# A written-out order for chunks 1 to 7 of a sort-attention and gated-MLP kernel, with seven units' scores and two value groups on 64 rows of TensorE

## Chip, cores, metric

One Trainium2 chip, one of its cores. The metric is the device time of one execution in microseconds (us), as the median of the runs shown. All matmul operands are bfloat16, all products are collected in float32 in PSUM, and the result is float32.

## What is computed

Attention over blocks that a Sinkhorn-normalized matrix has mixed, followed by a two-layer MLP with a gate. Cut to what matters:

```python
# q, k, v: (4, 8, 768, 64) = batch, heads, rows, width; sort_net: (4, 8, 8, 8)
P = sort_net
for _ in range(5):
    P = exp(P - P.max(-1)); P = P / (P.sum(-1) + 1e-9); P = P / (P.sum(-2) + 1e-9)
k_sorted = einsum('bhij,bhjcd->bhicd', P, k_blocks)     # 8 blocks of 96 rows
v_sorted = einsum('bhij,bhjcd->bhicd', P, v_blocks)
scores = (q_block @ k_sorted_block.T) / sqrt(64)        # 96 x 96 in each block and head
attn = softmax(scores)
x = attn @ v_sorted                                     # -> 3072 tokens x 512
h = x @ w_in                                            # 512 -> 2048
out = (h * cos(h)) @ w_out                              # 2048 -> 512
```

## The kernel before

**Chunks.** The 3072 tokens are worked off in 8 chunks of 384 (`TC`); chunk n is half of batch n // 2. A chunk has 4 units u of 96 tokens (one block of all 8 heads). Chunks 0 to 3 use the sorted keys and values of the first two batches (`kT`, `vS[0]`), chunks 4 to 7 those of the last two (`kT2`, `vS[1]`, which lies in the tile `pair`). While the MLP of chunk n runs, the attention of chunk n + 1 is put between its products. The sorted keys and values of the later batches are made in pieces between those products as well.

**The steps of one unit.** The scores are 8 matmuls (`scores`, L403, shown as L405), one for each head: the stationary operand is 128 columns of the transposed queries, the streamed one 96 columns of keys. Two heads share the 128 rows of a tile. `q_turned` holds each head's 64 rows with zeros in the other 64, so every matmul uses all 128 rows. VectorE (DVE) takes the maximum (L447) and subtracts it (L449; chunk 1 uses L698 and L702). ScalarE (ACT) takes the exponential into one of three buffers `p_bufs` (`expo`, L462, shown as L467). The result is transposed, on TensorE in chunks 0 and 1 and for one unit of chunk 2, else by a DMA that SyncE's queue (SP) issues (L480), into `pT`. Then come 8 value products (`av_products`, L502, shown as L514), the division by the row sums on DVE (`av_norm`, L525 and L527), and a second transposition into `xT`, on TensorE (L545) or by SP's DMA (L533). A half-score (`qk_half`) is the same for one head of each pair, 4 matmuls.

**The MLP of one chunk.** `up` (L551) makes 2 of 16 row groups of h with 8 matmuls of 384 columns (L558); ACT computes cos (L562), DVE multiplies (L566). 8 such steps are one chunk. `down` (L578) then makes the 128-token output tiles ts = 0, 1, 2 with 16 matmuls of 512 columns each (L583); a half is 8 of them, and some work is put behind the fourth one of a half (`mid`).

**Sorting.** `k_sort_g` (L378) makes 4 column groups of the late keys with 4 matmuls (L375) and one copy. `v_sort_b` (L411) makes 8 columns of the values of batch 1 (L415); `v_sort_g` (L422) makes 4 or 8 columns of the last two batches' values (L425: 128 rows, 128 streamed columns each), and a copy puts them into `vS[1]`. `k_swap` (L387) moves half of the keys to the other 64 rows by two DMAs of SP's queue; the scores of chunk 2 need those of the first swap, and the scores of chunk 4 need those of the second.

**What sets the order.** The pools run under `tc.manual_schedule()`: each engine does its instructions in the order in which the program emits them, and each waits by semaphores for what it reads and for the buffer that it writes. PSUM has three buffers of two banks (pool `big`: up, full scores, value products, most transposes) and two of one bank (pool `acc`: output tiles, half-scores, most sorting). A new tile needs a buffer whose last reader is done. In the code from L782 the calls of chunk 0 and of the attention of chunk 1 stand one by one; from L981 on, helpers with slots (`moe_up`, `moe_down`, `ahead`) emit a step of the MLP and then what is listed for its slot. In these helpers the parts of a step are bound together: `qk` emits scores, maximum and subtraction in one go, `up` its products, cosine and gate, `av` the products and the division.

GpSimd (POOL) issues the loads, permutes the value columns (`v_permute`, L169) and has three "holds" (L484, L393): one-element copies that make the loads behind them wait for an earlier reader.

Of the kernel before, what the change touches and what calls it, by code (L numbers as in the profile page):

```python
# [14 lines left out]
AX = mybir.AxisListType  # L15


@with_exitstack
def kernel(
# [15 lines left out]
    nc = tc.nc  # L35
# [336 lines left out]
    MH = H2 * IC  # L372

    def k_products(ps, t, c, rows, rhs, keys=kbuf):
        nc.tensor.matmul(  # L375
            ps[:, t], keys[rows, c * 2 * D:(c + 1) * 2 * D], rhs, start=True, stop=True)

    def k_sort_g(t0, eng, pool, tag):  # L378
        ps = pool.tile([128, 4, 4 * NB], FP32, name="ks", tag=tag)
        for t in range(4):  # L380
            k_products(ps, t, t0 + t, slice(0, 128), bds[1].rearrange("p x i -> p (x i)"),
                       pair)
        copy_on(
            eng, kT2[:, ::2, :, :, t0:t0 + 4].rearrange("p e b m t -> p b e m t"),
            ps.rearrange("p t (b e m) -> p b e m t", b=2, e=2))

    def k_swap(keys):  # L387
        nc.sync.dma_start(out=keys[:64, 1], in_=keys[64:, 0])
        nc.sync.dma_start(out=keys[64:, 1], in_=keys[:64, 2])

    def hold_keys():

        nc.gpsimd.tensor_copy(held[:], kT[1][:, 1, 0, :1])  # L393
# [14 lines left out]
    def v_cols(d, permuted):  # L408
        return vperm[:, d * blk:d * blk + 128] if permuted else vv[:, d]

    def v_sort_b(b, d0, nd, eng, pool, tag):  # L411
        ps = pool.tile([128, nd, 2 * NB], FP32, name="vs", tag=tag)
        rows, xs = slice(0, 64 + b * 64), slice(b * H, (b + 1) * H)
        for t in range(nd):
            nc.tensor.matmul(  # L415
                ps[:, t], v_cols(d0 + t, b == 1 or d0 + t >= D // 2)[rows],
                bdv[rows, xs].rearrange("p x i -> p (x i)"), start=True, stop=True)
        copy_on(
            eng, vS[0][:, b * 2 * NB:(b + 1) * 2 * NB, d0:d0 + nd],
            ps[:blk].rearrange("p t n -> p n t"))  # L420

    def v_sort_g(d0, nd, eng, pool, tag):  # L422
        ps = pool.tile([128, nd, 4 * NB], FP32, name="vs", tag=tag)
        for t in range(nd):
            nc.tensor.matmul(  # L425
                ps[:, t], v_cols(d0 + t, True), bds[1].rearrange("p x i -> p (x i)"),
                start=True, stop=True)
        copy_on(eng, vS[1][:, :, d0:d0 + nd], ps[:blk].rearrange("p t n -> p n t"))

    def v_at(g, b2, hp, h2, i):  # L430
        return (b2 * 2 + hp) * NB + h2 * nb + i


    LATE = 5
    s_t, pb, pT, xn_t = {}, {}, {}, {}
    xT = {}
    cnt = [0]

    def qk_part(n, u, part, pool, tag):
        w = len(part)  # L440
        sc = pool.tile([128, w, 512], FP32, name="sc", tag=tag)
        for h2 in range(H2):
            for e, hp in enumerate(part):
                scores(sc[:, e, h2 * 128:h2 * 128 + blk], n, u, h2, hp)
        scv = sc[:blk].rearrange("p e (h c) -> p (e h) c", c=128)[:, :, :blk]
        mx = small.tile([blk, w * H2], FP32, name="mx", tag="mx")
        nc.vector.reduce_max(mx[:], scv, axis=AX.X)  # L447
        s = s_t[n, u][:, part[0]:part[0] + w].rearrange("p e h c -> p (e h) c")
        nc.vector.tensor_tensor(s, scv, mx.to_broadcast(list(s.shape)), op=ALU.subtract)  # L449

    def qk(n, u):

        s_t[n, u] = sp.tile([blk, 2, H2, blk], FP32, name="s", tag="s")
        qk_part(n, u, [0, 1], big, "big")

    def qk_half(n, u, hp, pool=None, tag="acc"):

        if hp == 0:
            s_t[n, u] = sp.tile([blk, 2, H2, blk], FP32, name="s", tag="s")
        qk_part(n, u, [hp], pool or acc, tag)  # L460

    def expo(n, u, on_pe=False):  # L462
        p = p_bufs[cnt[0] % NP]
        cnt[0] += 1


        nc.scalar.activation(  # L467
            p[:, :, :blk], s_t.pop((n, u)).rearrange("p e h c -> p (e h) c"), AF.Exp,
            scale=scale)
        if n < LATE:  # L470
            t = ptp.tile([128, 2 * H2, blk], BF16, name="pT", tag="pT")
        else:

            z, w = (n * IC + u) % 8, 2 * H2 * blk
            t = vperm[:, z * w:(z + 1) * w].rearrange("p (a c) -> p a c", c=blk)
        pT[n, u] = t
        if on_pe:
            pb[n, u] = p
        else:
            nc.sync.dma_start_transpose(out=t[:], in_=p.rearrange("p a c -> p (a c)"))  # L480

    def hold(t):

        nc.gpsimd.tensor_copy(held[:blk], t[:blk, 0, :1])  # L484

    def p_hold(n, u):
        hold(pT[n, u])

    def p_transpose(n, u, eng, pool, tag):
        p = pb.pop((n, u))  # L490
        ps = pool.tile([128, 2 * H2, 128], BF16, name="pps", tag=tag)
        for a in range(2 * H2):
            nc.tensor.transpose(ps[:blk, a, :blk], p[:, a, :blk], ident[:blk, :blk])
        copy_on(eng, pT[n, u][:blk], ps[:blk, :, :blk])

    av_ps = {}

    def av(n, u, on_pe=False):
        av_products(n, u)
        av_norm(n, u, on_pe)  # L500

    def av_products(n, u):  # L502
        g, b2, ih = where(n)
        if n not in xT:
            xT[n] = xtp.tile([128, KC, TC], BF16, name="xT", tag="xT")
        a = big.tile([128, 2, 512], FP32, name="av", tag="big")
# [12 lines left out]
        av_ps[n, u] = a  # L519

    def av_norm(n, u, on_pe=False):
        avv = av_ps.pop((n, u))[:blk, :, :H2 * (D + 1)].rearrange(
# [3 lines left out]
        xn = small.tile([blk, H2, 2, D], BF16, name="xn", tag="xn")  # L526
# [3 lines left out]
        if on_pe:  # L530
            xn_t[n, u] = xn
        else:
            nc.sync.dma_start_transpose(  # L533
                out=xT[n][:, :, u * blk:(u + 1) * blk],
                in_=xn.rearrange("p h e d -> p (h e d)"))

    def x_transpose(n, u, eng, pool, tag, to=None):
        us = range(u, (u if to is None else to) + 1)
        ps = pool.tile([128, KC, len(us), blk], BF16, name="xps", tag=tag)

        turn = order[:] if n < NQ else ident[:blk, :blk]
        for i, z in enumerate(us):
            xn = xn_t.pop((n, z))
            for h2 in range(H2):
                nc.tensor.transpose(  # L545
                    ps[:, h2, i], xn[:, h2].rearrange("p e d -> p (e d)"), turn)
        copy_on(eng, xT[n][:, :, u * blk:us.stop * blk], ps.rearrange("p k i c -> p k (i c)"))

    gt = {}

    def up(n, fp):  # L551
        w = TC

        h = big.tile([128, 2, 512], FP32, name="h", tag="big")
        for f2 in range(2):
            f = fp * 2 + f2
            for kk in range(KC):
                nc.tensor.matmul(  # L558
                    h[:, f2, :w], w_in_t[:, kk, f * 128:(f + 1) * 128], xT[n][:, kk],
                    start=(kk == 0), stop=(kk == KC - 1))  # L560
        c = cosp.tile([128, 2, TC], FP32, name="c", tag="c")
        nc.scalar.activation(c[:], h[:, :, :w], AF.Sin, bias=half_pi[:, 0:1])  # L562
        if fp % 2 == 0:
# [576 lines left out]
```

## Time and profile before

| | |
|---|---|
| median of 3 runs | 238.28 us (238.25, 238.28, 240.16) |
| span of the profiled execution, first to last instruction | 236.9 us |
| median less span | 1.4 us |
| TensorE (PE) busy | 228.3 us, 96% of the span |
| VectorE busy | 171.1 us, 72% |
| ScalarE busy | 154.0 us, 65% |
| GpSimd busy | 93.4 us, 39% |
| matmuls | 2230 |
| read from and written to HBM | 27.27 MB, 6.29 MB |
| granted TensorE clock, mean of the span | 0.998 |

The profiled execution has no time of its own beside its span; what lies around the span is 1.4 us if it ran as the median did. In the profile, a matmul's row shows when it started and when its last result is taken to be written, so matmuls in a row overlap in time. What one costs in a row of them is the distance between starts. "Idle" of PE is therefore less than what is lost: a pause shorter than a matmul's tail is not seen as idle. The chain of waits cuts the overlap out and is the better place to read the cost of a group of matmuls.

### The profile page before, as it was taken

The page shows a single profiled execution, that of the slowest core. Times are in us where ns is not written, and L with a number is a line of the kernel's source. Part 1 is how long each engine was busy: PE and PEld are TensorE (multiplying, and loading weights), DVE is VectorE, ACT ScalarE, POOL GpSimd, SP SyncE. Part 2 cuts the span into 40 slices and gives each one's busy share as a digit, 9 for nine tenths or more (in the row PEclk, how much of TensorE's full clock was granted, in tenths as well). Part 3 has the DMA queues.
Part 4 walks back from the last instruction along what each step waited for, and adds up shares of the span by engine and source line. Part 5 has one row for each costly group of instructions (what it writes and reads, how often), then busy time and mean ns, then how long its engine had stood idle before and what let it go on. Part 6 is the DMA issues. An engine that isn't in the chain of part 4 may idle for free.

```text
span 236.9 us, 5429 instructions
## 1 busy us (share of the span) xinstructions
PE 228.3 (96%) x2230; PEld 144.0 (61%) x2230; DVE 171.1 (72%) x284; ACT 154.0 (65%) x205; POOL 93.4 (39%) x117
## 2 busy tenths in 40 slices
PE   8699999999999999999999999999999999999994
PEld 2368799567665656655666556655564565555553
DVE  5658976887789666893689976998698769535700
ACT  3356975588889747795688747673767376646611
POOL 7699994894970098940808000800000000000000
PEclk9999999999999999999999999999999999999999
DMA  7999999995899989869899938944972460341012
GB/s 97 203 199 205 203 224 211 148 201 167 102 117 183 146 155 136 160 150 184 95 104 101 116 64 150 209 68 91 119 216 46 80 192 3 55 133 47 0 44 89
DMA packets 66423, 30.89 MB, mean 130 GB/s; under 512 B 55136, under 2 KB 61920, under 8 KB 66144
## 3 DMA queue, kind: packets, MB, share of 16 engines
q0 software_dynamic: 24048, 13.64, 42.1%
q1 hardware_dynamic: 42064, 16.73, 33.4%
q8 instruction: 17, 0.28, 0.5%
q10 hardware_dynamic: 288, 0.20, 0.3%
q14 instruction: 6, 0.05, 0.1%
HBM read 27.27 MB, written 6.29 MB: 142 GB/s over the span
## 4 chain that ended last, share of the span: by engine, by line
PE 81%; DMA 6%; ACT 4%; DVE 4%; issue 3%; POOL 1%; SPq 0%; ACTq 0%; POOLq 0%
PE h L558 31%; PE o L583 21%; DMA pT<-p_buf 5%; PE h L735 5%; PE o L756 4%; PE sc L405 3%; PE av L514 3%; PE ks L375 2%; PE vs L662 2%; ACT p_buf L467 2%; PE o L1104 1%; PE vs L425 1%; PE pps L713 1%; DMA xT<-xn 1%; PE vs L238 1%
## 5 line engine op out<-in xcount | busy, mean ns | idle before, releaser
L558 PE MATMUL h<-xT,w_in_t 128*128 128x384 bf16 x448 | 78.4, 326 | 0.2 <-DMA xT<-xn 0.2
L583 PE MATMUL o<-w_out_t,gg 128*128 128x512 bf16 x320 | 76.5, 379 | 0.0
L566 DVE TENSOR_TENSOR gg<-c,h 128x768 bf16<-128x768 f32 x56 | 52.6, 949 | 18.8 <-ACT c L562 18.8
L562 ACT ACTIVATE c<-h,half_pi 128x768 f32<-128x768 f32 x56 | 50.4, 900 | 22.5 <-PE h L558 21.6
L558 PEld LDWEIGHTS <-w_in_t 128*128 128x128 bf16 x448 | 42.2, 98 | 26.5 <-issue 0.6
L583 PEld LDWEIGHTS <-gg 128*128 128x128 bf16 x320 | 29.1, 98 | 27.6
L467 ACT ACTIVATE p_buf<-s 96x768 bf16<-96x768 f32 x32 | 26.0, 840 | 4.4 <-DVE s L702 2.4
L179 POOL COPY vperm<-kv 64x1536 bf16<-64x1536 bf16 (+1 forms) x10 | 28.0, 2831 | 0.6 <-DMA kv<-in_v_dram 0.6
L449 DVE TENSOR_TENSOR s<-sc,mx 96x384 f32<-96x384 f32 (+1 forms) x33 | 24.3, 735 | 1.8
L447 DVE TENSOR_REDUCE mx<-sc 96x4 f32<-96x384 f32 (+1 forms) x33 | 24.0, 729 | 0.7 <-PE sc L405 0.7
L527 DVE TENSOR_TENSOR xn<-av,r 96x512 bf16<-96x512 f32 x32 | 22.0, 687 | 1.1
L525 DVE RECIPROCAL r<-av 96x8 f32<-96x8 f32 x32 | 6.4, 199 | 14.6 <-PE av L514 14.4
L129 POOL DMA_DIRECT2D kv<-in_q_dram x24 | 15.9, 674 | 0.7 <-issue 0.5
L405 PE MATMUL sc<-kTs,q_turned 128*128 128x96 bf16 x224 | 15.3, 206 | 0.1
L249 ACT COPY kv<-o 128x512 f32<-128x512 f32 (+2 forms) x10 | 5.3, 530 | 14.9 <-PE o L583 12.4
L405 PEld LDWEIGHTS <-q_turned 128*128 128x128 bf16 x224 | 12.6, 98 | 4.0 <-DVE s L449 0.4
L249 ACT CAST kTs<-ks 128x512 bf16<-128x512 f32 (+1 forms) x18 | 11.0, 632 | 5.7 <-PE ks L375 5.7
L756 PE MATMUL o<-w_out_t,gg 128*128 128x512 bf16 x48 | 11.4, 379 | 0.0
L251 DVE COPY kv<-o 128x512 f32<-128x512 f32 (+1 forms) x5 | 3.0, 602 | 11.4 <-PE o L1104 8.5
L129 POOL DMA_DIRECT2D q_mem<-in_q_dram x16 | 10.7, 684 | 1.2 <-DMA kv<-in_v_dram 1.0
L238 PE MATMUL idle<-warm 128*128 128x512 bf16 x29 | 8.5, 436 | 2.8 <-ACT q_turned L321 1.8
L735 PE MATMUL h<-xT,w_in_t 128*128 128x192 bf16 x128 | 11.1, 246 | 0.0
(119 smaller groups left out, 285.0 us busy)
## 6 DMA issues: line engine op xcount, KB each, us to landing
out_dram<-kv SPq DMA_DIRECT2D x12, 256.0 KB, 2.5
out_dram<-o_s SPq DMA_DIRECT2D x10, 256.0 KB, 2.7
w_in_t<-in_moe_w_in_dram POOLq DMA_DIRECT2D x4, 512.0 KB, 11.8
w_out_t<-in_moe_w_out_dram POOLq DMA_DIRECT2D x4, 512.0 KB, 12.6
kv<-in_k_dram POOLq DMA_DIRECT2D x2, 768.0 KB, 10.3
kv<-in_v_dram POOLq DMA_DIRECT2D x2, 768.0 KB, 13.1
pair<-in_k_dram POOLq DMA_DIRECT2D x2, 768.0 KB, 11.0
kv<-in_v_dram POOLq DMA_DIRECT2D x6, 256.0 KB, 5.4
```

The lines of the kernel that those rows point to most:

```text
L129: nc.gpsimd.dma_start(out=q_heads[:, i, :, e], in_=src[:, ih * IC + i, :, e])
L179: nc.gpsimd.tensor_copy(dst, src)
L405: nc.tensor.matmul(out, q_of(n, hp)[:, x:x + 128], keys_of(n, u, h2, hp), start=True, stop=True)
L447: nc.vector.reduce_max(mx[:], scv, axis=AX.X)
L449: nc.vector.tensor_tensor(s, scv, mx.to_broadcast(list(s.shape)), op=ALU.subtract)
L467: nc.scalar.activation(p[:, :, :blk], s_t.pop((n, u)).rearrange("p e h c -> p (e h) c"), AF.Exp, scale=scale)
L527: nc.vector.tensor_tensor(xn.rearrange("p h e d -> p e h d"), avv[:, :, :, :D], r.to_broadcast([blk, 2, H2, D]), op=ALU.mult)
L558: nc.tensor.matmul(h[:, f2, :w], w_in_t[:, kk, f * 128:(f + 1) * 128], xT[n][:, kk], start=(kk == 0), stop=(kk == KC - 1))
L562: nc.scalar.activation(c[:], h[:, :, :w], AF.Sin, bias=half_pi[:, 0:1])
L566: nc.vector.tensor_tensor(gt[n, fp // 2][:, f:f + 2], c[:], h[:, :, :w], op=ALU.mult)
L583: nc.tensor.matmul(o[:], gt[n, f // 4][:, f % 4, ts * 128:(ts + 1) * 128], w_out_t[:, f, :], start=(f == 0), stop=(f == FC - 1))
L735: nc.tensor.matmul(o[:, part, f2 * w:(f2 + 1) * w], w_in_t[:, kk, f * 128:(f + 1) * 128], xT[0][:, kk, h * w:(h + 1) * w], start=(kk == 0) ...
```

## The change

Chunk 0 and all that is emitted before its output products stays. What follows is no longer emitted by helpers with slots, but by a list, `PLAN`, of one word for each piece of work: S scores, M maximum, X subtraction, E exponential (with the number of its buffer), TD transposition by DMA, TP and TE by TensorE and its copy, AV and N value products and division, XD, XP and XE the second transposition, U, C, G an up step's products, cosine and gate, D a quarter (4 matmuls) of an output tile, O its copy out of PSUM, W its store, kg/kge, vb/vbe, vg/vge the sorting products and their copies, kswap and QD the swaps and query transposes on SP's queue, Lq, Lpv and hp/hq the loads and holds on POOL. "B" and "c" name the pools `big` and `acc`, "A" and "V" the engine of a copy; "nop" does nothing. The pieces of one step can so be set apart, and pieces of other steps between them.

- The order of the DMAs on SP's queue and of everything on POOL is the old one, word for word. The set of pieces is the old one but for the points below. The order on PE, VectorE and ScalarE is changed in many places from the output products of chunk 0 on; the first are chunk 1's maxima and sums, the last is up step 6 and 7 of chunk 7.
- `T` takes the place of `S` for the scores of seven units: (3,3), (4,3), (5,0), (6,0), (6,1), (7,2), (7,1). Each head's matmul uses its own 64 rows alone, and the two heads of a pair alternate. (4,3) and (5,0), (6,0) and (6,1), (7,2) and (7,1) stand next to each other on PE.
- `vgT` takes the place of `vg` for the value groups 0 and 2 (8 columns each): 16 matmuls of 64 rows and 64 streamed columns in place of 8 of 128 and 128. They stand ahead of and behind unit (3,3), so that there are four places with 64-row products.
- Five copies change engine or pool: the copy of key group 0 (`kse 0`) and of value group 0 (`vge 0`) go from ScalarE to VectorE, `XE 3 1` and the output copy `O 5 2` change engine (VectorE to ScalarE), and `XP 3 2` goes from `big` to `acc`.

```diff
+    def T(n, u, pool, tag):
+        o = kept_tile(("s", n, u, None), pool, tag, [128, 2, 512], FP32, "sc")
+        for h2 in range(H2):
+            for hp in range(2):
+                rows, x = slice(hp * D, (hp + 1) * D), (u * H2 + h2) * blk
+                nc.tensor.matmul(
+                    o[:, hp, h2 * 128:h2 * 128 + blk], q_of(n, hp)[rows, x:x + 128],
+                    keys_of(n, u, h2, hp)[rows], start=True, stop=True)
...
+    def vgT(z, nd, pool, tag):
+        o = kept_tile(("vg", z), pool, tag, [128, 2, nd, 2 * NB], FP32, "vs")
+        for t in range(nd):
+            for b in range(2):
+                rows = slice(b * 64, (b + 1) * 64)
+                nc.tensor.matmul(
+                    o[:, b, t], v_cols(z * 4 + t, True)[rows],
+                    bds[1][rows, b * H:(b + 1) * H].rearrange("p x i -> p (x i)"),
+                    start=True, stop=True)
```

The orders on PE at the places of which the prediction speaks (the first: on the engine of the copy), before and after, in the words of the list; a word without a sign stands in both:

```diff
 kse 5 V                                  (key copies ahead of the first swap)
-kse 0 A
+kse 0 V
 kswap 0
...
 D 1 0 2                                  (output products of chunk 1)
-kg 0 c / D 1 0 3 / S 2 3 B / kg 1 B / D 1 1 0 / D 1 1 1 / kg 2 B / AV 2 0 / kg 4 B / D 1 1 2 / D 1 1 3
-kg 3 B / AV 2 1 / TP 2 3 c / D 1 2 0 / D 1 2 1 / AV 2 2 / XP 2 1 B / AV 2 3 / XP 2 0 c / D 1 2 2
+S 2 3 B / kg 0 c / D 1 0 3 / kg 1 B / D 1 1 0 / D 1 1 1 / kg 4 B / D 1 1 2 / AV 2 0 / kg 2 B / D 1 1 3
+kg 3 B / AV 2 1 / TP 2 3 c / AV 2 2 / D 1 2 0 / XP 2 1 B / D 1 2 1 / AV 2 3 / XP 2 0 c / D 1 2 2
 kg 5 B / XP 2 2 B / XP 2 3 B / D 1 2 3
...
 D 2 0 3                                  (output products of chunk 2)
-S 3 3 B / vg 0 8 B / D 2 1 0 / D 2 1 1 / vg 2 8 B / D 2 1 2 / D 2 1 3 / AV 3 0 / AV 3 1 / vg 4 8 B
-D 2 2 0 / D 2 2 1 / AV 3 2 / AV 3 3 / vg 6 8 B / D 2 2 2 / XP 3 1 B / XP 3 2 B / XP 3 3 B / D 2 2 3
-U 3 0 / vg 8 4 c / S 4 0 c 0 / U 3 1
+vgT 0 8 B / T 3 3 B / vgT 2 8 B / D 2 1 0 / D 2 1 1 / D 2 1 2 / D 2 1 3 / AV 3 0 / AV 3 1
+D 2 2 0 / AV 3 2 / D 2 2 1 / AV 3 3 / vg 6 8 B / D 2 2 2 / XP 3 1 B / XP 3 2 c / XP 3 3 B / D 2 2 3
+U 3 0 / vg 8 4 c / vg 4 8 B / U 3 1 / S 4 0 c 0
...
 S 4 2 B / D 3 0 0 / D 3 0 1              (output products of chunk 3)
-S 4 3 B / D 3 0 2 / D 3 0 3 / vg 15 4 B / S 5 0 B / D 3 1 0
+T 4 3 B / T 5 0 B / D 3 0 2 / D 3 1 0 / vg 15 4 B / D 3 0 3
 D 3 1 1 / AV 4 0 / D 3 1 2 / D 3 1 3 / AV 4 1 / AV 4 2 / D 3 2 0 / D 3 2 1 / XP 4 1 B 2 / AV 4 3
...
 D 4 0 0 / D 4 0 1                        (output products of chunk 4)
-S 6 0 B / D 4 0 2 / D 4 0 3 / AV 5 0 / D 4 1 0 / D 4 1 1 / S 6 1 B / D 4 1 2 / AV 5 1 / D 4 1 3 / AV 5 2
-D 4 2 0 / D 4 2 1 / AV 5 3 / S 6 2 B / D 4 2 2 / XP 5 3 B / D 4 2 3
+D 4 0 2 / T 6 0 B / T 6 1 B / D 4 0 3 / AV 5 0 / D 4 1 0 / D 4 1 1 / D 4 1 2 / AV 5 1 / AV 5 2 / D 4 1 3
+D 4 2 0 / AV 5 3 / D 4 2 1 / D 4 2 2 / XP 5 3 B / D 4 2 3 / S 6 2 B
 U 5 0
...
 D 5 1 0 / D 5 1 1 / AV 6 2               (output products of chunk 5)
-S 7 1 B / D 5 1 2 / D 5 1 3 / AV 6 3 / D 5 2 0 / D 5 2 1 / S 7 2 B / D 5 2 2 / XP 6 3 B / D 5 2 3
+T 7 2 B / T 7 1 B / D 5 1 2 / AV 6 3 / D 5 1 3 / D 5 2 0 / D 5 2 1 / XP 6 3 B / D 5 2 2 / D 5 2 3
```

On VectorE in chunk 4's output products the subtraction `X 6 1` moves behind the divisions `N 5 1` and `N 5 2`, and with it the exponential `E 6 1` on ScalarE. The loop at the end of the kernel (the last output tile of chunk 7) is unchanged.

1651 lines of the change are left out of this document (1083 added, 568 removed).

## The prediction, made before the change was run

> **What bounds the kernel now.** I read the page first (busy times, groups), then PE's own rows for pauses, then the chain of waits and SP's rows around each pause.
>
> ```profile
> span 236.9 us, 5429 instructions
> ...
> PE 228.3 (96%) x2230; PEld 144.0 (61%) x2230; DVE 171.1 (72%) x284; ACT 154.0 (65%) x205; POOL 93.4 (39%) x117
> ...
> L558 PE MATMUL h<-xT,w_in_t 128*128 128x384 bf16 x448 | 78.4, 326 | 0.2 <-DMA xT<-xn 0.2
> ```
>
> PE is the bound: 96% busy, and its largest group, the up products at 78.4 / 448 = 175 ns each, is neither shortened nor made smaller. So the change can win only pauses of PE and the few matmuls that it halves. A pause is the distance between two starts less the work between them (columns: start, length with its tail, instruction, count):
>
> ```profile
> 62.68 0.40 PE L415 MATMUL vs<-bdv,vperm 128*128 128x64 bf16 x8
> 63.18 0.33 PE L405 MATMUL sc<-kTs,q_turned 128*128 128x96 bf16 x4
> ...
> 74.89 1.03 PE L583 MATMUL o<-w_out_t,gg 128*128 128x512 bf16 x4
> 75.94 0.33 PE L375 MATMUL ks<-bd,pair 128*128 128x128 bf16 x3
> ...
> 86.27 0.34 PE L545 MATMUL xps<-order,xn 96*128 96x96 bf16 x4
> 86.87 0.34 PE L545 MATMUL xps<-order,xn 96*128 96x96 bf16 x4 [0.27 <-DVE xn L527]
> ...
> 91.13 1.46 PE L558 MATMUL h<-xT,w_in_t 128*128 128x384 bf16 x8
> 92.53 0.38 PE L375 MATMUL ks<-bd,pair 128*128 128x128 bf16 x4
> ...
> 108.91 0.68 PE L514 MATMUL av<-vS,pT 96*128 96x65 bf16 x16
> 109.94 0.61 PE L425 MATMUL vs<-bd,vperm 128*128 128x128 bf16 x8 [0.34 <-ACT pair L249]
> ...
> 113.93 0.91 PE L545 MATMUL xps<-ident,xn 96*128 96x96 bf16 x12
> 114.68 1.03 PE L583 MATMUL o<-w_out_t,gg 128*128 128x512 bf16 x4
> ...
> 139.12 0.51 PE L545 MATMUL xps<-ident,xn 96*128 96x96 bf16 x8
> 140.03 0.43 PE L514 MATMUL av<-pair,pT 96*128 96x65 bf16 x8 [0.41 <-DMA pT<-p_buf]
> ...
> 165.35 1.03 PE L583 MATMUL o<-w_out_t,gg 128*128 128x512 bf16 x4
> 166.55 0.48 PE L558 MATMUL h<-xT,w_in_t 128*128 128x384 bf16 x2 [0.17 <-DMA xT<-xn]
> ```
>
> The work comes from pieces of the chain, which have no overlap (start, length, what):
>
> ```profile
> 73.85 0.86 PE o L583 x4
> 74.71 0.34 PE sc L405 x8
> ...
> 79.70 0.26 PE av L514 x8
> ...
> 112.78 0.46 PE vs L425 x8
> ...
> 141.67 0.17 PE xps L545 x4
> ```
>
> A quarter tile is 0.86 us, a unit's scores 0.34, its value products 0.26, its second transpose 0.17, a group of eight value columns 0.46; an up step is 8 x 0.175 = 1.40 by its group, and 1.30 by distance where nothing waits (91.13 + 1.30 = 92.43). The pauses: 0.27 ahead of the first score of chunk 2 (0.50 less half of 0.46 for eight products of half the columns), then 0.19 (1.05 - 0.86), 0.43 (0.60 - 0.17), 0.10 (1.40 - 1.30), 0.51 (1.03 - 2 x 0.26), 0.24 (0.75 - 3 x 0.17), 0.57 (0.91 - 0.34), 0.34 (1.20 - 0.86). That is 2.65 us. Ahead of chunk 1's first up step are some tenths more, which I leave out: the same chain of division, transpose and copy stands there after the change. The head and the tail keep theirs.
>
> **The 64-row products.** Chunk 0 has 64-row scores already, with the two row halves alternating:
>
> ```profile
> 20.57 0.40 PE L681 MATMUL sc<-kTs,q_turned 64*128 64x64 bf16 x14
> 20.91 0.39 PE L238 MATMUL vs<-warm 128*128 128x512 bf16 x1
> 21.23 0.93 PE L662 MATMUL vs<-bdv,vperm 64*128 64x128 bf16 x14
> ```
>
> Less a last tail of about 0.2 (0.33 for four scores that take 0.17), 14 of them start within 0.2 us, 16 ns each for 48 to 64 columns; full-row scores take 0.34 / 8 = 42 ns for 96, so 26 for 60. Pairs do overlap. For a `T` I take a pair in the time of one, 0.17 us instead of 0.34; for a `vgT` 16 products at 16 ns, 0.26 instead of 0.46. The price stands in the same rows: 512 columns take 0.32 (20.91 to 21.23), though four times as many take 0.86; and from the last L681 at about 20.78 to 20.91 are 0.13, of which 0.03 are its own columns. So a visit to 64 rows costs 0.1 on each side. The first of the four (two groups, one unit) saves 0.40 + 0.17 - 0.20 = 0.37, each of the others 0.34 - 0.20 = 0.14: 0.8 us of PE's work. Ends: 1.6 saved if no side costs anything, 0.8 lost if no pair overlaps. I take 0.8 saved; both halves of it are in these rows.
> The Trainium skill, "TensorEngine Tiling (Array Packing)", section Tiling Modes, states the rule that speaks against this: a change of the tiling mode, not of the tile alone, drains TensorE. By its promise of up to twice the speed alone the saving would be 1.6 us; with the drains of the rows 0.8. By that rule, the trace agrees.
>
> **Chunk 1 (60 to 88 us): 0.1 lost.** The score at 63.18 waits for the key swap:
>
> ```profile
> 60.08 0.59 SPq L389 DMA_DIRECT2D kTs<-kTs  x1
> ...
> L249 ACT CAST kTs<-ks x4: 585/598/618, 57.3 to 58.9; 128x512 bf16<-128x512 f32 x4
> L251 DVE CAST kTs<-ks x1: 691/691/691, 58.5 to 58.5; 128x512 bf16<-128x512 f32 x1
> ...
> DMA to landing us min/median/max: 2.8/2.9/3.0
> ```
>
> 60.08 + 3.0 is 63.1. The swap goes out when the last key copy is done, 58.9 + 0.6 = 59.5 on ScalarE. Now that copy runs on VectorE behind the other (58.5 + 0.69 = 59.2), to about 59.8: 0.2 to 0.3 later, and PE has nothing to put there. I count 0.2 (ends 0 and 0.5, if the copy ahead starts late too).
> In the output products the scores of unit 3 fill the 0.19, and unit 2's value products go ahead of two quarters, so that unit 3's division is early and the 0.43 goes. But these products need a DMA transpose:
>
> ```profile
> 82.91 0.18 POOL L484 CAST held<-pT 96x1 f32<-96x1 bf16 x1 [13.18 <-DMA pT<-p_buf]
> ...
> 84.33 0.42 PE L514 MATMUL av<-vS,pT 96*128 96x65 bf16 x8
> ```
>
> It lands just ahead of the hold at 82.91. PE used to come at 84.33; now it comes at 84.33 - 2 x 0.86 - 0.19 + 0.2 = 82.6, and the transpose, which hangs on the last up step, lands at 82.9 + 0.2 = 83.1. So 0.5 of waiting takes the place of 0.62, and with the swap's 0.2 about 0.1 is lost. Behind the waiting products stands all of PE's queue.
>
> **Chunk 2 and up steps (88 to 117 us): nothing.** The half-score's subtraction now runs ahead of the gate, which takes away the 0.10, and by the same edit I count 0.1 in chunk 3's up steps. The 0.51 (a value group whose buffer ScalarE still reads) goes: that group moves behind the next up step, and another one's copy goes to VectorE. The 0.24 goes by a buffer of the other pool. But chunk 3's last value products wait for SP's queue:
>
> ```profile
> 103.71 2.56 SPq L480 DMA_TRANSPOSE pT<-p_buf  x2
> 106.36 1.31 SPq L573 DMA_DIRECT2D out_dram<-o_s  x1
> 107.85 2.58 SPq L480 DMA_TRANSPOSE pT<-p_buf  x2
> ...
> 112.23 0.18 POOL L484 CAST held<-pT 96x1 f32<-96x1 bf16 x1 [9.12 <-DMA pT<-p_buf]
> ```
>
> From the first transpose to the fourth, SP's queue pauses for under 0.2 us, and its order is kept. The fourth lands at 112.2; its products started 112.78 - 0.26 - 0.17 = 112.35 or so. So what PE saves ahead of them (the 0.51, the 0.37 of the first visit, the group moved away) turns into a wait there, but for 0.1. Behind it, 0.24 go and the moved group's 0.46 come: 0.1 won in the up steps, 0.1 lost in the rest.
>
> **Chunk 3 (117 to 143 us): 0.1 won,** in its up steps. The second visit's 0.14 lies ahead of the wait at 140.03, which hangs on one transpose:
>
> ```profile
> 135.62 4.37 DMA pT<-p_buf
> ```
>
> Its exponential waits for the buffer of the first transpose, in the old order, and the work between the last up step and these products is the same set as before. The 0.57 grows to 0.7.
>
> **Chunk 4 (143 to 167 us): 0.3 won.** Unit 2's value products, now directly behind unit 1's, come one quarter and the third visit's saving earlier (0.86 + 0.14), and the subtraction of unit (6,1), which stood ahead of their division on VectorE, goes behind it. So the `xT` transpose of unit 2 goes out at least 0.8 earlier, and the 0.34 at 166.55, a wait for it, goes. The products themselves come to wait 0.2 for this:
>
> ```profile
> 156.57 3.88 SPq L480 DMA_TRANSPOSE vperm<-p_buf  x3
> ...
> vperm<-p_buf SPq DMA_TRANSPOSE x12, 2.9
> ```
>
> The second issue is at 156.57 + 3.88 / 3 = 157.9 and lands at 160.8 or a little later. The wait of 0.2 eats the third visit's 0.14.
>
> **Chunk 5 to the end: 0.14 won** by the fourth visit, which stands behind the wait for its transposes. Chunks 6 and 7 have no pause to win. Other moved pieces I cost at nothing: on VectorE and ScalarE they lie beside PE's work (72% and 65% busy); without that cover a copy costs 0.6 to 0.7.
>
> **Sum.** +0.1 + 0 - 0.1 - 0.3 - 0.14 = -0.45 us: span 236.5, and with the 1.4 us by which the median of the runs shown (238.28) is above the profiled span, **237.8 us**.
>
> **Rivals.** First, earlier transposes (0.15): if the one of 4.37 us lands like the others (2.9), 0.7 go in chunk 3, and if chunk 1's comes 0.5 earlier, so does its wait: 237.8 - 1.2 = 236.6. For it: one of 12 is an outlier, which may not come back; against it: the queue's order is kept. Second, the new order wins all (0.10): 238.28 - 2.65 - 0.8 = 234.8. For it speaks that each pause has an edit; against it that three of the edits end at a transpose. Third, slower (0.13): value products brought ahead of output quarters wait with PE's whole queue behind them. In chunk 1 their margin goes from 84.33 - 82.91 = 1.4 us to none; if that transpose lands as late as the one of 4.37, 1.5 us later, all of it is PE's: 237.8 + 1.5 = 239.3. It decides once the landing slips by over 0.45. Fourth, the change doesn't do what it says (0.17): the 64-row pairs gain nothing with their drains, or all four visits lie ahead of waits, and the pauses only change places: 238.3, between 238.0 and 238.6.
>
> **Chances and range.** The forecast has 0.45 (237.3 to 238.1). One per cent, 2.4 us, is about what a measurement tells from no change. Only the second rival is under 235.9, and a part of the first if it meets others: faster 0.12. Over 240.7 only the third with several late transposes: slower 0.03. Within: 0.85. The range, 235.7 to 239.5, leaves out the second rival's whole win and the far end of the third.
>
> **What would show it.** Right: the first score of chunk 2 waits 0.4 to 0.6 for the swap; unit (2,2)'s value products follow its transpose's landing at once; a wait of 0.6 to 0.8 ahead of unit (4,3)'s value products and one of the same kind ahead of unit (3,3)'s; no pause ahead of chunk 5's up steps; eight `T` starts within 0.2 us with 0.1 on each side. Wrong: PE without pauses around the transposes, or pauses of over 0.3 us where none is named here.

## The result, and the profile after

| | before | after |
|---|---|---|
| median of 5 runs each | 238.58 us (238.25 to 240.16) | 240.97 us (240.40 to 241.37) |
| after / before | | 1.0096, 95% interval 1.0066 to 1.0125 |
| span of the profiled execution | 236.9 us | 239.1 us |

The forecast was 237.8 us, between 235.7 and 239.5. The change makes the kernel 1% slower, in its profiled span by 2.2 us. What lies around the span grew too: the time of a run less its span is 2.1 us in the runs of after, and 1.8 us in those runs of before for which both are listed (1.72 to 1.96 in all runs of the old order below, 2.08 to 2.27 in all of the new one). The traces don't show why. The page of after, its first lines and the group of the up products:

```profile
span 239.1 us, 5437 instructions
...
PE 227.2 (95%) x2224; PEld 142.3 (60%) x2246; DVE 172.2 (72%) x284; ACT 153.1 (64%) x205; POOL 93.5 (39%) x117
...
L1505 PE MATMUL h<-xT,w_in_t 128*128 128x384 bf16 x448 | 78.4, 326 | 0.4 <-DMA xT<-xn 0.4
```

PE is busy for 1.1 us less (some matmul records are missing) and the span is 2.2 us longer: PE waits more. The up products take 78.4 us as before. What PE waits for stands in the view of PE's waits (us in total, times, longest). The rows of before that concern a transposition by DMA are these two:

```profile
PE av L514 <- DMA pT<-p_buf: 0.4, 1, 0.4
...
PE h L558 <- DMA xT<-xn: 0.2, 1, 0.2
```

and after:

```profile
PE av L1445 <- DMA pT<-p_buf: 2.2, 3, 1.4
...
PE av L1445 <- DMA vperm<-p_buf: 1.0, 1, 1.0
PE h L1505 <- DMA xT<-xn: 0.4, 1, 0.4
PE sc L1344 <- DMA kTs<-kTs: 0.3, 1, 0.3
```

(L1445 is L514, L1505 is L558; `vperm` holds the transposed probabilities from chunk 5 on.) Waits for transpositions grow from 0.6 to 3.6 us, 3.0 more; all the rest is 0.8 shorter. Where they are, PE's rows of after show (start, length, instruction, in brackets the idle time ahead and what ended it):

```profile
63.37 0.33 PE L1344 MATMUL sc<-kTs,q_turned 128*128 128x96 bf16 x4 [0.28 <-DMA kTs<-kTs]
...
82.23 0.54 PE L1427 MATMUL pps<-ident,p_buf 96*96 96x96 bf16 x8
82.83 0.43 PE L1445 MATMUL av<-vS,pT 96*128 96x65 bf16 x8
...
111.15 0.43 PE L1445 MATMUL av<-vS,pT 96*128 96x65 bf16 x8 [1.37 <-DMA pT<-p_buf]
...
137.38 0.43 PE L1445 MATMUL av<-pair,pT 96*128 96x65 bf16 x8 [0.36 <-DMA pT<-p_buf]
138.28 0.43 PE L1445 MATMUL av<-pair,pT 96*128 96x65 bf16 x8 [0.47 <-DMA pT<-p_buf]
...
166.61 0.51 PE L1344 MATMUL sc<-kTs,q_turned 128*128 128x96 bf16 x8
167.50 1.79 PE L1505 MATMUL h<-xT,w_in_t 128*128 128x384 bf16 x10 [0.38 <-DMA xT<-xn]
...
187.36 0.43 PE L1445 MATMUL av<-pair,vperm 96*128 96x65 bf16 x8 [1.00 <-DMA vperm<-p_buf]
```

These are, in order: unit (2,0)'s first score, unit (2,2)'s value products, units (3,2), (4,1) and (4,2), the scores ahead of chunk 5's first up step and that step, unit (6,3). The wait that was forecast ahead of unit (4,3) is not there. The chain of waits over three of these places names what came late (start, length, what):

```profile
134.25 3.98 DMA pT<-p_buf
138.23 0.05 issue
138.28 0.43 PE av L1445 x8
...
163.73 3.63 DMA xT<-xn
167.36 0.14 issue
167.50 1.62 PE h L1505 x9
...
182.82 4.49 DMA vperm<-p_buf
187.31 0.04 issue
187.36 0.43 PE av L1445 x8
```

From issue to landing, a transposition of probabilities mostly takes 2.8 to 3.0 us where nothing meets it, one into `xT` 2.3; here they took 4.0, 4.5 and 3.6. Before had such late ones too, but others: the 4.37 at 135.62 that the prediction quotes was one. It was no exception. Of the 33 transpositions of before into `pT`, `vperm` and `xT` from 72 us on, 10 landed over 0.6 us late, 5 of them among the 11 into `pT`, whose times before are, in the view of that tile:

```profile
DMA to landing us min/median/max: 2.8/3.0/4.5
```

**What else moves at that moment.** The DMA view of 185 to 186 us of after: the DMA engines' busy share in 40 slices of 25 ns, the packets, and the queues' share of 16 engines' time.

```profile
DMA  9953320000000000000000000000000000002458
...
DMA packets 123, 0.04 MB, mean 41 GB/s; under 512 B 122, under 2 KB 122, under 8 KB 122
...
q1 hardware_dynamic: 122, 0.02, 13.6%
q8 instruction: 1, 0.02, 5.8%
```

While a transposition of SP's queue (q1) is under way, one packet of another queue, "q8 instruction", holds one DMA engine: 5.8% of 16 engines in 1 us is 0.93 us of one engine. Beside it, all other engines stand still (a zero is under a tenth of the 16) until it is done, and only then the rest of the transposition moves (2458). The whole kernel has 17 such packets, before and after:

```profile
q8 instruction: 17, 0.28, 0.5%
```

0.28 MB / 17 is 16 KB a packet. In the traces they come about every 125 weight loads of PE (2258 records of loads before, the 17 packets between load 170 and 2147), so a packet holds some 250 instructions of PE, loads and matmuls; that they are PE's is read from this spacing, and the shifts below bear it out. The Trainium skill, "Runtime: NRT & Kernel Launch", section Instruction fetch mechanics, says the same of the size (an engine's instruction store is refilled in blocks of 16 KiB, 256 instructions, by a DMA queue of its own) and that the cost of crossing a block is mostly hidden. On the size the traces agree; "hidden" does not hold for a transposition that is in flight. In after, packets start at 108.16, 135.30, 163.68 and 185.04 us, each in the flight of the transpositions on which the four groups of waits above hang; before, at 106.04, 137.93, 167.70 and 185.05, where they met, among others, the transpositions of units (3,0), (4,3) and (6,0), and the second one of (6,0); of these only (4,3)'s made PE wait. The DMA view of before from 137.5 to 139 us has the same standstill:

```profile
DMA  9999999986490000000000345989899998754320
...
q8 instruction: 1, 0.02, 3.7%
```

By stage (start of the first cosine of a chunk on ScalarE, to the next; the order of these is the same in all kernels; s20 is explained below):

| stage | before | after | forecast of the change | measured | s20 |
|---|---|---|---|---|---|
| chunk 1, first up step of 2 | 28.29 | 28.26 | +0.1 | 0.0 | 28.25 |
| chunk 2 | 27.63 | 27.34 | 0 | -0.3 | 26.72 |
| chunk 3 | 27.01 | 27.89 | -0.1 | +0.9 | 26.71 |
| chunk 4 | 23.99 | 24.38 | -0.3 | +0.4 | 23.92 |
| chunk 5 to the end | 68.9 | 70.1 | -0.14 | +1.2 | 68.8 |

### The profile page after: what moved, and what is told of

It is laid out like the page before. It is cut to its first block, busy times and chain, and to the rows that moved or that the text cites. A ratio compares the mean times of both kernels' runs of the same rounds, so it can differ in the third digit from the quotient of the medians.

```text
span 239.1 us, 5437 instructions
## 1 busy us (share of the span) xinstructions
PE 227.2 (95%) x2224; PEld 142.3 (60%) x2246; DVE 172.2 (72%) x284; ACT 153.1 (64%) x205; POOL 93.5 (39%) x117
## 4 chain that ended last, share of the span: by engine, by line
PE 72%; DMA 10%; DVE 9%; ACT 5%; issue 2%; SPq 1%; POOL 1%; ACTq 0%; POOLq 0%; DVEq 0%
PE h L1505 29%; PE o L1550 21%; DMA pT<-p_buf 5%; PE h L1528 4%; PE av L1445 3%; PE vs L1281 2%; PE sc L1344 2%; DMA vperm<-p_buf 2%; ACT p_buf L1403 2%; DMA xT<-xn 2%; DVE s L1399 2%; DVE mx L1385 1%; PE xps L1479 1%; PE o L1641 1%; PE ks L1225 1%
## 5 line engine op out<-in xcount | busy, mean ns | idle before, releaser
L1550 PE MATMUL o<-w_out_t,gg 128*128 128x512 bf16 x349 | 84.2, 379 | 1.2 <-issue 0.3
L1505 PE MATMUL h<-xT,w_in_t 128*128 128x384 bf16 x448 | 78.4, 326 | 0.4 <-DMA xT<-xn 0.4
L1505 PEld LDWEIGHTS <-w_in_t 128*128 128x128 bf16 x448 | 42.1, 98 | 26.2 <-issue 0.5
L1550 PEld LDWEIGHTS <-gg 128*128 128x128 bf16 x368 | 33.3, 98 | 33.3 <-DVE gg L1517 0.3
L1385 DVE TENSOR_REDUCE mx<-sc 96x8 f32<-96x768 f32 (+1 forms) x41 | 31.6, 771 | 4.4 <-PE sc L1344 3.4
L1094 ACT COPY kv<-o 128x512 f32<-128x512 f32 (+2 forms) x11 | 5.9, 535 | 12.2 <-PE o L1550 9.6
L1344 PEld LDWEIGHTS <-q_turned 128*128 128x128 bf16 x168 | 9.8, 98 | 3.5 <-issue 0.4
L1344 PE MATMUL sc<-kTs,q_turned 128*128 128x96 bf16 x168 | 11.6, 206 | 0.3 <-DMA kTs<-kTs 0.3
L1083 PE MATMUL idle<-warm 128*128 128x512 bf16 x28 | 9.8, 498 | 2.1 <-ACT q_turned L1166 1.0
L1094 ACT COPY xT<-xps 128x384 bf16<-128x384 bf16 (+1 forms) x11 | 5.5, 506 | 9.0 <-PE xps L1479 9.0
L1445 PEld LDWEIGHTS <-pT 96*128 96x128 bf16 (+1 forms) x160 | 7.2, 101 | 6.0 <-DMA pT<-p_buf 4.2
```

The costliest lines, as they stand in the source:

```text
L1094: eng.copy(dst, src)
L1344: nc.tensor.matmul(out, q_of(n, hp)[:, x:x + 128], keys_of(n, u, h2, hp), start=True, stop=True)
L1385: nc.vector.reduce_max(mx[:], s_view(n, u, hp), axis=AX.XY if n < 2 else AX.X)
L1505: nc.tensor.matmul(o[:, f2, :TC], w_in_t[:, kk, f * 128:(f + 1) * 128], xT[n][:, kk], start=(kk == 0), stop=(kk == KC - 1))
L1550: nc.tensor.matmul(out_ps[n, ts][:], gt[n, q][:, f % 4, ts * 128:(ts + 1) * 128], w_out_t[:, f, :], start=(f == 0), stop=(f == FC - 1))
```

## The experiments

Theory A: the packets of PE's instructions hold up whatever transposition is in flight; the change moves the packets (by 32 PE instructions that the two `vgT` add, and by the order), and the new order reads some transpositions with no margin. Theories B: the order by itself (B1), or the 64-row products by themselves (B2), cost the time wherever the packets fall. "Waits" in the table is the sum of the rows `av <- DMA` and `h <- DMA` of PE's waits in the profiled execution; "rest" is the span less the start of chunk 1's first cosine less these waits. Ratios are to runs of before on the same chip, taken together with the kernel's own; the medians come from several chips, so the ratios are the better comparison.

| kernel | order, rows | PE instructions more, at the head | median us | ratio, 95% interval | span | waits | rest |
|---|---|---|---|---|---|---|---|
| before | old, full | 0 | 238.58 | | 236.9 | 0.6 | 175.2 |
| e4_before_shift | old, full | 78 | 238.94 | 0.9973, 0.9947 to 0.9998 | 237.4 | 0.9 | 174.9 |
| o20 | old, full | 40 | 240.51 | 1.0059, 1.0040 to 1.0078 | 238.7 | 2.5 | 175.1 |
| e2_rows | old, 64 | 0 | 241.66 | 1.0101, 1.0066 to 1.0136 | 239.6 | 3.1 | 175.4 |
| e6_rows_shift | old, 64 | 78 | 238.70 | 0.9975, 0.9949 to 1.0001 | 237.1 | 1.0 | 174.8 |
| r20 | old, 64 | 40 | 239.06 | 0.9994, 0.9978 to 1.0011 | 236.9 | 0.8 | 175.0 |
| e1_order | new, full | 0 | 238.98 | 0.9999, 0.9969 to 1.0029 | 237.7 | 2.4 | 174.1 |
| e8_order_16 | new, full | 32 | 240.48 | 1.0069, 1.0048 to 1.0090 | 238.4 | 2.5 | 174.8 |
| f20 | new, full | 40 | 239.41 | 1.0006, 0.9990 to 1.0023 | 237.2 | 1.5 | 174.6 |
| e7_order_shift | new, full | 78 | 237.75 | 0.9951, 0.9928 to 0.9974 | 235.6 | 0.4 | 173.9 |
| after | new, 64 | 0 | 240.97 | 1.0096, 1.0066 to 1.0125 | 239.1 | 3.6 | 174.4 |
| s20 | new, 64 | 40 | 237.61 | 0.9931, 0.9906 to 0.9957 | 235.5 | 0.7 | 173.7 |
| e3_after_shift | new, 64 | 78 | 238.02 | 0.9947, 0.9923 to 0.9971 | 235.6 | 0.8 | 173.6 |
| s64 | new, 64 | 128 | 239.25 | 1.0000, 0.9961 to 1.0039 | 238.7 | 2.7 | 174.9 |
| s84 | new, 64 | 168 | 239.03 | 0.9985, 0.9948 to 1.0022 | 236.9 | 1.9 | 173.7 |
| s104 | new, 64 | 208 | 239.88 | 1.0028, 1.0001 to 1.0055 | 237.0 | 2.4 | 173.2 |
| e5_period | new, 64 | 256 | 240.88 | 1.0087, 1.0062 to 1.0113 | 238.7 | 3.3 | 174.0 |

The waits and the rest are those of one traced execution, the median is of all runs of a kernel, and these spread widely: before took 238.18 to 241.68 us in the 102 runs beside these kernels, e1_order 238.36 to 241.71. The traced run of s64 is the slowest of its ten (240.84 us), that of e1_order is 0.9 above its median, that of s104 0.7 below. Whether the packets also move from one run of a kernel to the next isn't shown.

**Order alone, rows alone, and the head shifted.** The first four:

```diff
e1_order, in the list of after
-vgT 0 8 B / T 3 3 B / vgT 2 8 B / T 4 3 B / T 5 0 B / T 6 0 B / T 6 1 B / T 7 2 B / T 7 1 B
+vg 0 8 B / S 3 3 B / vg 2 8 B / S 4 3 B / S 5 0 B / S 6 0 B / S 6 1 B / S 7 2 B / S 7 1 B
e2_rows, in before
+        half = w == 2 and (n, u) in ((3, 3), (4, 3), (5, 0), (6, 0), (6, 1), (7, 2), (7, 1))
+        (these scores as T makes them; v_sort_g of columns 0 and 8 as vgT does)
e3_after_shift in after, e4_before_shift in before
-    keep_warm(15, big.tile([128, 512], FP32, name="idle", tag="big"))
+    idle_ps = big.tile([128, 512], FP32, name="idle", tag="big")
+    keep_warm(2, idle_ps)
+    keep_warm(52, idle_ps, 128)
```

> The new order with all scores and value groups on full rows (S and vg in place of T and vgT): as many instructions of PE as before the change. Theory A (16 KB instruction packets on one DMA engine hold up the transposes that are in flight; the change moves these packets, by 32 more PE instructions and by the order): the packet that delayed the transposes of units (4,1) and (4,2) at 135.3 us comes 2 to 3 us later, after 137, and the waits ahead of the value products change place: 0 to 0.5 us ahead of units (4,1) and (4,2), and the wait of 1.17 ahead of unit (6,3) goes only if no packet falls between 183 and 186 us. Time 239 to 241. Theory B1 (the order alone is guilty, whatever the packets): the same waits at the same units as after the change, and PE's 0.8 us of 64-row savings lost: 241.0 to 241.8. Theory B2 (the 64-row products are guilty): 238.6 or less.

> The old order with the seven scores and the two value groups on 64 rows. Theory A: the packets come some 2 us earlier in chunk 2 and beyond than before the change; the wait of 0.57 ahead of unit (4,3) (packet at 137.9) goes or moves to (4,1), and the value products of the old order keep over 1 us of margin, so no new wait of over 0.5 us: 237.6 to 238.8. Theory B1 (order guilty): 237.8, the 0.8 us of saved products. Theory B2 (64-row products guilty): 240 to 241.

> The changed kernel with 13 of the 15 idle products of 512 columns at its head split into four of 128 each: same columns, 78 more PE instructions, nothing else. Theory A: every packet comes some 5 us earlier in the work; the ones at 135.3, 163.7 and 185.0 us fall to about 144 (behind the last transpose of chunk 3), 159 and 181.4, away from the transposes of units (4,1), (4,2), (5,1) and (6,3); the waits ahead of these (0.53, 0.65, 0.55, 1.17) go but for 0.3 each at most, and the time is 238.0 to 239.2. Theories B1, B2: the waits stay and the time is 240.8 to 241.2.

> The kernel before the change with the same split at its head. Theory A: the packet at 137.9 falls to about 134, into the transposes of units (4,0) to (4,2), which have 1 to 2 us of margin in the old order; the one delayed to 139.99 (unit (4,3)) lands at 138.5 and the wait of 0.57 there goes, unless the delay is passed on through the queue: 238.0 to 239.0, the waits in other places than before. Theories B1, B2: the profile and the time stay as before, 238.4 to 238.8, with the wait of 0.57 ahead of unit (4,3).

The third tells most: with the same work in the same order, 78 instructions in the idle head take 3 us off (240.97 to 238.02). Its rows for transpositions:

```profile
PE av L1447 <- DMA vperm<-p_buf: 0.6, 1, 0.6
...
PE av L1447 <- DMA pT<-p_buf: 0.2, 1, 0.2
```

The waits of 1.4 (chunk 2), 0.8 (chunk 3) and 1.0 (chunk 5) are gone but for 0.2, and one of 0.6 has come in chunk 4. B1 and B2 as whole explanations fall. The order alone is on a par with before, 0.02 below what A expected, with 2.4 us of waits. In detail A missed there: the packet at 135.3 did not move past 137 but stayed (135.19), and the waits ahead of units (4,1) and (4,2) are 1.05 and 0.53; one at 185.16 cost no wait ahead of unit (6,3), whose transposition was about to land (185.34). The rows alone were a miss: A gave 237.6 to 238.8, and 241.66 came. I had taken a margin of over 1 us for the old order; a late transposition is 1.5 late, and two of them were met:

```profile
136.07 0.43 PE L534 MATMUL av<-pair,pT 96*128 96x65 bf16 x8 [0.99 <-DMA pT<-p_buf]
...
186.03 0.43 PE L534 MATMUL av<-pair,vperm 96*128 96x65 bf16 x8 [1.47 <-DMA vperm<-p_buf]
```

(units (4,0) and (6,2), with packets at 133.94 and 183.98 us). So the old order is no protection. e4_before_shift pays 0.5 us at its head (chunk 1's first cosine at 61.62 and not 61.12) and wins 0.4 in chunk 3, where the wait at unit (4,3) is gone, and 0.5 in chunk 2; it loses 0.5 in chunk 4, with 0.7 of waiting for an `xT` transposition, and 0.3 behind it.

**A whole packet, and both halves shifted.** Is it the split of the idle products that helps? With 256 instructions more, the packets should fall as without any. The edits: in after, `keep_warm` splits its first products into five (narrower ones into two) until 128 are added (e5_period, and with other numbers the s kernels, o20, r20 and f20); e6 and e7 are e2 and e1 with the head of e3; e8_order_16 splits five products into four and one into two.

```diff
+    more = [128]
     def keep_warm(times, t, cols=512):
         for _ in range(times):
-            nc.tensor.matmul(
-                t[:, :cols], warm[:], warm[:, :1].to_broadcast([128, cols]),
-                start=True, stop=True)
+            n = 1 + min(more[0], 4 if cols == 512 else 1)
+            more[0] -= n - 1
+            for i in range(n):
+                a, z = i * cols // n, (i + 1) * cols // n
+                nc.tensor.matmul(
+                    t[:, a:z], warm[:], warm[:, :1].to_broadcast([128, z - a]),
+                    start=True, stop=True)
```

> The changed kernel with its idle products of chunk 0 split so that PE gets 256 more instructions of 64 bytes in all (128 products, 128 weight loads), which is one whole packet of 16 KB; the columns are the same. Theory A (it counts where the packets fall): one packet more is fetched, and the others fall on the same work as after the change, to 20 weight loads or so: the waits ahead of the value products of units (4,1), (4,2) and of (6,2) or (6,3) come back, 240.3 to 241.8. Rival (split idle products help by themselves, at the head or through the clock): as fast as with 78 instructions more, 237.5 to 238.7.

> The old order with 64-row scores and value groups, and the 78 instructions more at the head. Theory A: the packets that stood at 133.9, 164.4 and 184.0 us come 4 to 5 us earlier in the work; the waits of 1.0 ahead of unit (4,0), 0.6 for xT in chunk 4 and 1.5 ahead of unit (6,2) go: 238.0 to 239.4, and under the shifted kernel before (238.94) by up to 0.8 if the 64-row products save what the prediction took. Theory B2 (64-row products slow the old order by themselves): 241 to 242.

> The new order with full rows and the 78 instructions more at the head. Theory A: no packet on the transposes of chunks 3 and 5; 237.8 to 239.0, and above the changed kernel with the same 78 (238.02) by what the 64-row products save, 0.3 to 0.8. Theory B1 (order guilty): 240 to 241.

> The new order with full rows and 32 instructions more at the head, as many as the two 64-row value groups add: from chunk 2 on the packets fall on the same work as after the change, to 20 weight loads or so. Theory A: a packet near 185 us on the transposes of units (6,2) and (6,3) and one on those of chunk 3, waits of 0.5 to 1.2 there: 240 to 241.7. Theory B2 (the 64-row products are guilty, not the packets): as without the 32, 238.4 to 239.2.

All four came as A has it, e7 0.05 below its range. After one whole packet more, the time of after is back (240.88), and so are its waits, nearly row by row:

```profile
PE av L1451 <- DMA pT<-p_buf: 2.3, 3, 1.4
...
PE av L1451 <- DMA vperm<-p_buf: 1.0, 1, 1.0
```

The 64-row products in the old order lose 3 us of their cost when shifted (241.66 to 238.70), and the order with full rows, which was on a par with before, becomes slower with 32 instructions more (240.48) and faster with 78 (237.75). In e8_order_16 the chain shows unit (6,3)'s transposition again, and its packet:

```profile
182.19 4.49 DMA vperm<-p_buf
```

```profile
q8 instruction: 1, 0.02, 5.3%
```

(the second line is of its DMA view from 184.3 to 185.4 us). One part of e7's expectation failed: it is not 0.3 to 0.8 above e3 but level with it.

**Other shifts, and the parts at one small shift.**

> The changed kernel with 40 instructions more of PE in chunk 0 (20 products, 20 loads; idle products split, columns the same). Theory A: the packets come 20 weight loads earlier in the work than after the change; they stay on the first transposes of chunks 3 and 5 (132 to 134 and 183 to 184.5 us): 240.0 to 241.2. Rival (any split helps, the more the better): between 238.0 and 240.97 in line with the number, about 239.4.

> The same with 128 instructions more. Theory A: packets near 113, 141, 157 and 190 us, where no transpose is under way whose readers stand next on PE: 237.5 to 238.8. Rival (the more the better): 238.0 or less, and s104 lower still.

> The same with 168 instructions more. Theory A: packets near 111, 139.8 and 187.5 us, on second transpositions and query transposes, which are read an up step or more later: 237.6 to 239.2.

> The same with 208 instructions more. Theory A: packets near 108.4, 137.5 and 185 us, on the last transposes of chunk 2's and 3's attention and on the second transpositions of chunk 5: 239.2 to 241.0. Rival (the more the better): under 238.0.

> The kernel before the change with 40 instructions more in chunk 0, as in s20. Theory A, with the sum of the prediction as the worth of the order: the packets fall on about the same loads as in s20 (1239, 1498, 1783, 1890, between the transposes of chunks 3 and 5); the old order then loses its own late transposes too (units (3,0) and (4,3)): 237.8 to 238.6, 0.3 to 1.0 above s20 (237.61). Rival (all of s20's gain is the place of the packets, the order is worth nothing): within 0.2 of s20.

> The new order with full rows and 40 instructions more: against s20 (237.61) only the 64-row products are undone. Each double visit saves 0.11 us at its place by the traces of the two shifted kernels, the whole some 0.6. If that reaches the end: 238.1 to 238.3. If it only lengthens the wait for the transposes behind it: 237.5 to 237.8.

> The old order with the 64-row products and 40 instructions more. Theory A: packets some 30 loads earlier than in the kernel with 64-row products alone (241.66); the waits ahead of units (4,0) and (6,2) go: 237.6 to 239.0, and within 0.3 of the old order with full rows at the same shift. Theory B2 (64-row products slow the old order by themselves): over 240.

s20 was expected slow and is the fastest of all, o20 was expected near s20 and is slow, and s64, f20 and r20 (by 0.06) are outside too; r20 was also expected within 0.3 of o20, and is 1.45 below it. What failed is foreseeing where the packets fall, not what they do. In the 17 traces, from 60 us on, PE waits 20 times for over 0.6 us for one of these transpositions, and in 18 of them that transposition had a q8 packet in its flight. The two others, in e4_before_shift (0.69) and o20 (0.89), are for an `xT` transposition that took the plain 2.3 us, but was issued right behind one that a packet had met. Shorter waits also stand ahead of transpositions at their plain price, as the 0.5 of s20. s20 has its packets at 129.4, 162.4 and 177.1 us, ahead of the transpositions of chunks 3 and 5 or on second ones. Its rows:

```profile
PE av L1451 <- DMA pT<-p_buf: 0.5, 1, 0.5
...
PE av L1451 <- DMA vperm<-p_buf: 0.2, 1, 0.2
```

and its DMA view from 178.5 to 193 us has no instruction packet, and transpositions at their plain price:

```profile
q1 hardware_dynamic: 4880, 1.87, 54.6%
...
vperm<-p_buf SPq DMA_TRANSPOSE x4, 2.9
xT<-xn SPq DMA_TRANSPOSE x3, 2.3
```

The rival "the more is split, the better" falls as well: 237.6, 238.0, 239.3, 239.0, 239.9, 240.9 for 40 to 256. Nor is it the opposite, for with none added it is 241.0, and the old order has 238.6, 240.5 and 238.9 with 0, 40 and 78.

**The ledger.** In the table the rest is 174.8 to 175.4 in all six kernels of the old order (mean 175.1, with full rows and with 64), 173.9 to 174.8 in the new order with full rows (mean 174.4) and 173.2 to 174.4 with 64 rows (mean 173.7; s64 left out, which also waits 1.3 us for a copy in chunk 1, not followed up). The waits run from 0.6 to 3.1 in the old order and from 0.4 to 3.6 in the new. So the new order is worth about 0.7 us and the 64-row products in it about 0.6, by means from which single kernels lie up to 0.6 off. For the 64-row products three pairs of kernels give 0.4 (after against e8_order_16), 0.9 (s20 against f20) and 0.3 (e3 against e7) of the rest; in the medians of these pairs the waits hide it (0.5 slower, 1.8 faster, 0.3 slower). About half of the order's 0.7 is lost again around the span, where the new order takes some 0.35 more in every kernel. Against before, after won 0.8 us of rest in its profiled run and paid 3.0 more in waits.

## Why the prediction was wrong, step by step

- **The premise that failed:** "From the first transpose to the fourth, SP's queue pauses for under 0.2 us, and its order is kept", and with it that each transposition lands as before if it is issued as before. Chunks 2 to 5 are costed on landings read from the trace of before. Issue and queue order did stay; the landings did not, since the late ones follow the instruction packets, and a list in another order with 32 PE instructions more has them elsewhere.
- **A term that was mis-sized:** the 1.4 us around the span. It set the span of one execution against the median of the runs; a run's own time less its own span is 1.8 before and 2.1 after. That is 0.7 of the 3.2 us between forecast and result; the rest is in the span (236.5 forecast, 238.8 in the run of the median time). The five stages, as the prediction adds them, make -0.44 and not -0.45, which changes nothing.
- **Chunk 3, 0.1 won:** 0.9 lost. "The 0.57 grows to 0.7" was tied to unit (4,3)'s transposition of 4.37 us as a fixed thing. It was the packet at 137.93. In after the packet at 135.30 hit those of units (4,1) and (4,2).
- **Chunk 4, 0.3 won:** 0.4 lost. The subtraction did move and unit (5,2)'s `xT` transposition went out earlier (0.9 by the stage's own time), but the packet at 163.68 held it up for 1.3, and the 0.34 became 0.55 (167.50 - 166.61 - 0.34).
- **Chunk 5, 0.14 won:** with the rest, 1.2 lost. No wait was forecast at unit (6,3); its products stand one quarter earlier than in the old order, and the transposition came 1.6 late. In s20 this stage is 0.1 faster than before, as forecast.
- **Chunk 2, nothing:** 0.3 won, by two errors that nearly cancel. The old late one (unit (3,0), which also delayed those behind it) went away, and a wait of 1.37 ahead of unit (3,2) came, again by a packet (108.16). In s20, with a wait of 0.5 there, 0.9 is won: the 0.51 and 0.24 of pauses were winnable.
- **Chunk 1, 0.1 lost:** nothing (0.03 won). The swap was right in size (63.37 and not 63.18; 0.2 forecast). Unit (2,2)'s products follow the landing at once, with 0.3 of waiting and not 0.5: 82.83 less the end of 8 transpositions at 82.23 + 0.34. That this landing came as forecast has some luck in it: a packet (78.36 before, 78.68 after) met that transposition both times; in e3, where none did, it landed 0.9 earlier.
- **64-row products, 0.8 of PE's work saved:** 0.6 by the ledger. A double visit, in the shifted kernels e7 (full rows) and e3 (64):

```profile
129.33 0.84 PE L1346 MATMUL sc<-kTs,q_turned 128*128 128x96 bf16 x16
130.01 1.89 PE L1552 MATMUL o<-w_out_t,gg 128*128 128x512 bf16 x8
```

```profile
128.76 0.38 PE L1552 MATMUL o<-w_out_t,gg 128*128 128x512 bf16 x1
129.07 0.54 PE L1373 MATMUL sc<-kTs,q_turned 64*128 64x96 bf16 x16
129.55 1.90 PE L1552 MATMUL o<-w_out_t,gg 128*128 128x512 bf16 x8
```

  0.68 us with full rows; with 64, from 128.76 + 0.216 (one output product) to 129.55, 0.57. It saves 0.11 where 0.14 was forecast, and 0.1 goes on each side, as taken from chunk 0. This is the drain that the Trainium skill, "TensorEngine Tiling (Array Packing)", section Tiling Modes, states; by that rule, the trace agrees. It would also explain why the same products gain nothing in the old order (rest 175.1 with and without): there the scores of (4,3) and (5,0) and the other pairs stand apart, and by the prediction's prices a lone unit saves 0.17 and pays 0.2. No run tests that by itself.
- **The rivals.** The third, "value products brought ahead of output quarters wait with PE's whole queue behind them", is the nearest: its place (chunk 1) was wrong, its effect (1.5 late, all of it PE's) came at units (3,2) and (6,3). Its cause was not the missing margin alone, for e2_rows and o20 pay as much in the old order. The first rival said that the outlier "may not come back"; it didn't, and others came. And "one of 12 is an outlier" misread the trace of before: 10 of 33 were late there, among them that of unit (2,2), on which chunk 1 was costed, and that of unit (3,0), which stands ahead of the others of chunk 2. The range was too narrow for want of asking what made them late.

Where the packets mostly leave the transpositions alone (s20, e3 and e7), the time is 237.6 to 238.0 us against the 237.8 forecast, but by luck: the span is 235.5 to 235.6 and not 236.5, above all since the waits that were to eat the wins of chunk 2 did not come in full (0.9 won in s20), and what lies around it is 2.1 to 2.2 and not 1.4. **Those three beat both kernels** (s20 by 0.7% of before, interval 0.4% to 0.9%); the same work at other shifts costs up to 3.4 us more.

## What to carry to other kernels

Before a landing in a trace is used as fixed, ask what made it what it is: where a transposition by DMA is 1.5 us over its fellows, look for an instruction packet in the DMA view of that moment (most such ones had one here), and expect that after an edit another may be met. Where matmuls read transpositions with under 1.5 us of margin, an edit worth under 1% can't be judged from one time: run it, and its rival, at two or three shifts of the instruction stream (idle products split in the head), and compare the span less the waits as well. And take what lies around the span from runs that list both. Products of 64 rows pay where several stand together, since each visit cost 0.1 us on each side here.

## What the runs showed of the hardware

- In the 17 profiled executions, from 72 us on, 561 transpositions of `pT`, `vperm` and `xT` were issued. With an instruction packet (q8, or q14, a second queue of that name) in their time of flight, from 0.9 us behind the issue to 0.2 ahead of the plain landing, 107 of 149 landed more than 0.6 us above the plain time (2.85 us, `xT` 2.35); without one, 10 of 412, of which 8 stood right behind a delayed one. With a q8 packet it is 100 of 125, with one of q14 alone (8 KB or less) 7 of 24. The bounds of the flight were chosen on these same traces. A q8 packet holds one engine for 0.9 to 1.8 us, once for 2.4. That one held part is what delays the whole is read from the traces; taking the packets away couldn't be tried.
- What sets a packet's place is open. Counted in PE's weight loads, the packets from 100 to 165 us come at about 1250, 1385, 1510, 1640 and 1770 in every kernel, up to 27 loads to either side. e8_order_16 and s20 differ by 4 loads at the head and by the 64-row groups, and have packets at loads 1525 and 1498, 1925 and 1890; their spans lie nearly 3 us apart, of which the 64-row products make 0.6.
